# Windowed attention and two feed-forward blocks on one core: the first tile's tap sums and all weight-part sums move to TensorE

## Chip, cores and metric

The kernel runs on one core of a Trainium2 chip. The metric is the device time of one execution in microseconds (us); lower is better. Engines are named as in the profile: PE (TensorE matmul), PEld (its weight loads), DVE (VectorE), ACT (ScalarE), POOL (GpSimd), SP (SyncE, which issues all the DMAs here).

## What is computed

Three stages follow each other for 2 batches of 4160 tokens of width 192:

```python
# 1: every token is a weighted sum of itself and the 6 tokens before it
w = softmax(weight_gen, over its 7 taps)           # per token, head (8) and tap (7)
out[b, s, h, g] = sum_k w[b, s, h, k] * x_pad[b, s + k, h, g]
# 2: mix with the token before, then a gated feed-forward block, d_ff = 1024
xk = mu_k * x + (1 - mu_k) * x_prev ; xr = mu_r * x + (1 - mu_r) * x_prev
y  = sigmoid(xr @ w_r) * (relu(xk @ w_k) ** 2 @ w_v)
# 3: a second feed-forward block with a 3-tap convolution along the tokens
h  = relu(y @ w_in) ; c = conv3(h, conv_w) ; result = (h * sigmoid(c)) @ w_out
```

The mixing rates, the projections and the convolution weights of stages 2 and 3 arrive as 64-bit or 32-bit floats. A 64-bit matrix is read as pairs of 32-bit words.

## The kernel before

**Tiles.** The 4160 tokens of a batch are cut into 10 tiles (`SIZES`: 256, 220, seven of 476, 352). A tile is done for both batches. The loop at the end of `conv_moe_kernel` gives tile i the plan time T = 16 i; within it `moe1` and `moe2` run over 8 slices of the 1024 hidden units for each batch, and `moe2` lags `moe1` by 10 plan units, so that stage 3 works on the tile before while stage 2 works on this one.

**Order of the work.** No engine order is written by hand. Each step puts closures with a plan time into `plan` (`at`, line 292); they run in order of that time and append instructions to `prog.ops`. `Program.schedule` (line 106) then plays all instructions through a table of costs (`cost`, line 77), takes on each engine the ready instruction with the smallest plan time, and emits each engine's instructions in the order that this play gives. Each engine executes its list strictly in that order, so a changed cost or a moved instruction can change the order anywhere behind it. SP's list holds all the DMA issues.

**Stage 1** (`attention`, line 452). A tile's tokens lie on 128 partitions, in 2 to 4 slots each; one slot of one batch is a "token" below. For a token POOL multiplies the seven rows `rows` by the softmax weights `sw` into `prod` (128x1344, seven taps of 192) and adds the taps in three steps, the last of which writes `tok` (lines 466 to 470). There is one `prod` buffer. Tile 0 has four tokens, tile 1 has four, tile 2 and the later ones eight. The softmax weights are made ahead by `softmax` (line 421): DVE folds, ACT takes the exponential, and POOL subtracts and multiplies, these being the POOL instructions that write `sw`.

**Mixing** (`mixing`, line 481). PE transposes `tok` into a `pa` bank ("flip", the rows `pa<-ident,tok`); ACT copies the shifted tokens into `att`, DVE forms the mixture into `ar` or `mk`, ACT rounds its high part into `xA` or `rm`, and the low part is the rest (DVE for tile 0, POOL for later tiles). For a tile's unit u = 2, which needs the tokens of both batches, SP moves the parts into `xB` by DMA. Stage 2 of a batch starts with the matmuls `pa<-xA,wkA` and `pa<-xB,wkB`.

**Weights.** Each large matrix product is done in three passes of reduced-precision float32 parts ("high" and "low"). `prepare` (line 400) brings the weights in as 16 chunks; `fetch` loads one into `stage` by DMA (three buffers), `narrow` (line 321) makes a float32 value of the 64-bit words in a PSUM bank `px` (`bm` and `br` in turn), and `split` (line 345) rounds it to a high part and keeps the rest as the low part. For the first three chunks (`on_pe`, line 409) the sum of the two parts inside `narrow` is two matmuls with an identity matrix, `ident` (float32) and `signs` (rounded), and the subtraction inside `split` is a matmul with the negative identity followed by an ACT copy. For the other 13 chunks both are DVE instructions (lines 342 and 351). The `chunk_*` functions that say where a chunk goes all end in `split`, but for the convolution weights (`chunk_conv`).

**Store** (`store`, line 733). The result of the 64 last channels of a tile is put together in its own buffer `ob` and stored by DMA.

Of the kernel before, what the change touches and what calls it, by code (L numbers as in the profile page):

```python
# [1 line left out]

# [12 lines left out]
NB, SEQ, DM, NH, KS, DFF = 2, 4160, 192, 8, 7, 1024  # L15
# [12 lines left out]
WIN = KS * DM  # L28
# [6 lines left out]
def f(ap):  # L35
    return ap.bitcast(F32)


class Program:
# [37 lines left out]
    def cost(self, eng, method, out, ins, pointer):  # L77

        n = self.count(out)
        src = [self.space(x) for x in ins]  # L80
        if method == "dma_start":
            return 0.6, 0.0
        if eng == "PE":
            if method == "matmul" and ins[0].dtype == F32:
                n *= 4
            busy = max(n * 0.00045 + 0.002, 0.109)
            return busy, busy + 0.24
        if eng == "ACT":
            near = bool(src) and src[0] == "PSUM"
            p = 0.1 if pointer else 0.0  # L90
            return (0.06 if near else 0.09) + p + n / 1200, (0.2 if near else 0.24) + p + n / 1200
        if eng == "DVE":
            if method == "tensor_reduce":
                return 0.05 + self.count(ins[0]) / 515, 0.15 + self.count(ins[0]) / 515
            if method == "reciprocal":
                return 0.07 + n / 160, 0.2 + n / 160
            if method in ("tensor_scalar", "tensor_copy", "memset") and "PSUM" not in src:
                return 0.07 + n / 1920, 0.2 + n / 1920
            stt = method == "scalar_tensor_tensor"
            return (0.13 if stt else 0.07) + n / 960, (0.26 if stt else 0.2) + n / 960  # L100
        if eng == "POOL":
            busy = 0.15 + (n / 455 if method == "tensor_tensor" else n / 270)
            return busy, busy + 0.1
        return 0.6, 0.6
# [85 lines left out]
def conv_moe_kernel(ctx: ExitStack, tc: tile.TileContext, xp, wg_first, wg_rest, mus, w_k, w_v, w_r, w_in, conv_w, w_out, out):  # L190
    nc = tc.nc
    prog = Program(nc)
    PE, ACT, DVE, POOL, SP = (prog.engine(e) for e in ("PE", "ACT", "DVE", "POOL", "SP"))
# [3 lines left out]
    def new(name, shape, dtype=F32):  # L197
        t = sb.tile(shape, dtype, name=name)
        prog.spaces[t.tensor.name] = "SBUF"
        return t  # L200

    def ring(name, n, shape, dtype=F32):
        return Ring([new(f"{name}{j}", shape, dtype) for j in range(n)])

    def bank(name):
        t = ps.tile([128, 512], F32, name=name)
        prog.spaces[t.tensor.name] = "PSUM"
        return t

    W = NMAX + 4  # L210
# [22 lines left out]
    ident = new("ident", [128, 128])  # L233
# [12 lines left out]
    stage = new("stage", [128, 4096], U32)  # L246
# [5 lines left out]
    g_r = ring("g", 2, [128, 2, W], F32R)  # L252
    wz_r = Ring([t.rearrange("p a b -> p (a b)") for t in g_r.tiles])
    rows_r = ring("rows", 2, [128, max(SLOTS) + PAD, DM])
    prod = new("prod", [128, WIN])
    tok_r = ring("tok", 2, [128, max(SLOTS), NB * DM])
    att_r = ring("att", 2, [128, NMAX])
    mk_r = ring("mk", 2, [128, NMAX])
# [4 lines left out]
    s_r = ring("s", 2, [128, 2, NMAX], F32R)  # L263
    h_r = ring("h", 2, [128, W])
    om_r = ring("om", 1, [128, W])
    ob_r = ring("ob", 1, [64, W])


    slots = [NB * l for l in SLOTS]
    soft_at = [sum(slots[:j]) for j in (0, 1, 2, 3, NTILE)]  # L270
# [2 lines left out]
    sm = []  # L273
    for j in range(4):
        n = soft_at[j + 1] - soft_at[j]
        flat = new(f"smz{j}", [128, 2 * n * NH]) if j < 3 else f(stage)[:, :2 * n * NH]
        sm.append((sw[:, soft_at[j]:soft_at[j + 1]],
                   *(flat[:, c * n * NH:(c + 1) * n * NH].rearrange("p (s h) -> p s h", s=n) for c in (0, 1))))
    pa_r = Ring([bank(f"pa{j}") for j in range(2)])
# [10 lines left out]
    plan = []  # L290

    def at(t, fn, hold=0.0):
        plan.append((t, len(plan), fn, hold))

    def mm(dst, passes):
        n = len(passes)
        for i, (w, r) in enumerate(passes):
            PE.matmul(dst, lhsT=w, rhs=r, start=(i == 0), stop=(i == n - 1))
# [20 lines left out]
    on_pe = [False]  # L319

    def narrow(st, n):
        if not st["wide"]:
            return st["x"][:, :n]
        hi, lo = st["raw"][:, :n, 1], st["raw"][:, :n, 0]
        px, py = px_r()[:, :n], py_r()[:, :n]
        x, y, z = px.bitcast(U32), py.bitcast(U32), wy_r()[:, :n]
        ACT.activation(px, f(hi), ACTF.Copy, scale=2.0 ** -112)
        if on_pe[0]:

            zr = wz_r()[:, :n]  # L330
            DVE.tensor_scalar(x, x, 3, None, op0=ALU.logical_shift_left)
            DVE.scalar_tensor_tensor(out=z, in0=hi, scalar=0x80000000, in1=x, op0=ALU.bitwise_and, op1=ALU.bitwise_or)
            DVE.tensor_scalar(y, z, 0xFF800000, None, op0=ALU.bitwise_and)
            DVE.scalar_tensor_tensor(out=zr, in0=lo, scalar=2.0 ** -52, in1=py, op0=ALU.mult, op1=ALU.mult)
            PE.matmul(px, lhsT=ident, rhs=f(z), start=True, stop=False, skip_group_check=True)
            PE.matmul(px, lhsT=signs[:, 0:128], rhs=zr, start=False, stop=True, skip_group_check=True)
            return px
        DVE.tensor_scalar(x, x, 3, None, op0=ALU.logical_shift_left)
        DVE.scalar_tensor_tensor(out=x, in0=hi, scalar=0x80000000, in1=x, op0=ALU.bitwise_and, op1=ALU.bitwise_or)
        DVE.tensor_scalar(y, x, 0xFF800000, None, op0=ALU.bitwise_and)  # L340
        DVE.scalar_tensor_tensor(out=f(z), in0=lo, scalar=2.0 ** -52, in1=py, op0=ALU.mult, op1=ALU.mult)
        DVE.tensor_tensor(px, px, f(z), op=ALU.add)
        return px
# [56 lines left out]
    def prepare(first, seq):  # L400

        for j, (t, (load, n, go)) in enumerate(seq):
            st = {}

            def ld(st=st, load=load):
                st[0] = load()

            def use(st=st, n=n, go=go, j=j):
                on_pe[0] = j < 3
                go(narrow(st[0], n))  # L410

            at(first[j] if j < 3 else seq[j - 3][0] + 0.001, ld)
            at(t, use)
# [36 lines left out]
    rows_t, tok_t = {}, {}  # L450

    def attention(i, b, t_load, t, dt_, eng, hold=(0.0, 0.0)):
        L = SLOTS[i]

        def load():
            rows_t[i, b] = rows_r()[:, :L + PAD]
            row = b * (SEQ + PAD) + STARTS[i] - EXTRA[i]
            SP.dma_start(out=rows_t[i, b], in_=bass.AP(tensor=xp.tensor, offset=xp.offset + row * DM, ap=[[L * DM, PART[i]], [1, (L + PAD) * DM]]))

        def token(l):  # L460
            if i not in tok_t:
                tok_t[i] = tok_r()
            p = prod
            y = p.rearrange("p (k d) -> p k d", k=KS)
            w = sw[:, sum(slots[:i]) + b * L + l].unsqueeze(2).to_broadcast([128, KS, DM // NH, NH])
            eng.tensor_tensor(p.rearrange("p (k g h) -> p k g h", k=KS, h=NH),
                              rows_t[i, b][:, l:l + KS].rearrange("p k (g h) -> p k g h", h=NH), w, op=ALU.mult)
            eng.tensor_tensor(y[:, 0:3], y[:, 0:3], y[:, 3:6], op=ALU.add)
            eng.tensor_tensor(y[:, 0:2], y[:, 0:2], y[:, 2:7:4], op=ALU.add)
            eng.tensor_tensor(tok_t[i][:, l, b * DM:b * DM + DM], y[:, 0], y[:, 1], op=ALU.add)  # L470

        at(t_load, load, hold[0])
        for l in range(L):
            at(t + l * dt_, lambda l=l: token(l), hold[1])
# [258 lines left out]
    def store(i, b, t):  # L733
        N = UNIT[i]
        last = i == NTILE - 1
        a = 1 if i == 1 else 0
        n = N + (1 if last else 0)
        t0 = STARTS[i] - OFFSET[i] - 1
        st = {}

        def e0():
            st["b"] = ob_r()
            ACT.copy(st["b"][:, :n], acc2["r"][64:128, :n])

        def e1():
            st["m"] = om_r()
            ACT.copy(st["m"][:, :n], acc2["m"][:, :n])
            SP.dma_start(out=out[b, 0:128, t0 + a:t0 + n], in_=st["m"][:, a:n])

        def e2():  # L750
            DVE.tensor_tensor(st["b"][:, :n], acc2["r"][0:64, :n], st["b"][:, :n], op=ALU.add)
            SP.dma_start(out=out[b, 128:192, t0 + a:t0 + n], in_=st["b"][:, a:n])

        at(t, e0)
        at(t + 0.1, e1)
        at(t + 0.2, e2)
# [36 lines left out]
    for j in range(NTILE - 3):  # L793
        a, b = (sum(slots[3:3 + k]) for k in (j, j + 1))
# [10 lines left out]
    for i in range(NTILE):  # L805
# [6 lines left out]
        for b in range(NB):  # L812
            t = T + 8 * b
# [8 lines left out]
            if i:  # L822
                store(i, b, t + LAG + 10.02)

    for t, _, fn, hold in sorted(plan, key=lambda e: e[:2]):
        prog.now, prog.hold = t, hold
        fn()
    with tc.manual_schedule():
# [64 lines left out]
```

## Time and profile before

| | |
|---|---|
| median of 3 runs | 766.72 us (765.65 to 767.09) |
| the profiled execution, own time | 766.81 us |
| its span in the profile | 765.0 us |
| PE busy | 697.2 us (91%) |
| ACT busy | 650.8 us (85%) |
| DVE busy | 621.6 us (81%) |
| POOL busy | 506.6 us (66%) |

The profiled execution's own time is 1.8 us longer than its span. Busy times are shares of the whole span; the program is a start-up of some 45 us, then ten tiles in a pipeline, then an end. "Idle before <- X" in a row means that the engine stood still ahead of that instruction, and that X ended last among what it needed. A row of several instructions (x2, x3) gives the time from the first's start to the last's end. A float32 matmul with `ident` shows as two matmul records.

### The profile page before, as it was taken

To read this page: it belongs to the slowest core of one execution; us is meant where nothing else is said; L and a number is where in the kernel's file an instruction comes from. 1 tells how busy PE (TensorE), PEld (TensorE's weight loads), DVE (VectorE), ACT (ScalarE), POOL (GpSimd) and SP (SyncE) were. 2 spreads that over 40 slices of the span, in tenths; PEclk is the share of its full clock that TensorE was granted. 3 is DMA by queue.
4 is the path that set the end of the run, shared out by engine and by line. 5 is a ranking of instruction groups with operands and counts; after the bars stand their busy time and mean duration, and the time that the engine had idled before them with its cause. 6 is when DMAs were issued, how large, how long until landed. Compare 5 with 4: busy or idle time off the path is not lost.

```text
span 765.0 us, 10294 instructions
## 1 busy us (share of the span) xinstructions
PE 697.2 (91%) x3358; PEld 590.4 (77%) x3358; DVE 621.6 (81%) x1066; ACT 650.8 (85%) x1364; POOL 506.6 (66%) x362
## 2 busy tenths in 40 slices
PE   4177888998899999999999899999999999999996
PEld 1066676887677888887888688888888888888984
DVE  5897868877997979796979587888787878787887
ACT  3477779988888999898989798999899989898886
POOL 4999999999899999999999999585602010110000
PEclk9999999999999999999999999999999999999999
DMA  7768103012210140112120310120002000200000
GB/s 239 224 174 250 53 1 103 20 53 71 51 53 20 51 122 4 69 52 71 51 72 9 110 53 20 47 71 1 20 0 71 1 19 2 58 0 20 20 1 28
DMA packets 18788, 45.05 MB, mean 59 GB/s; under 512 B 2992, under 2 KB 14256, under 8 KB 18608
## 3 DMA queue, kind: packets, MB, share of 16 engines
q1 hardware_dynamic: 18736, 44.41, 19.4%
q8 instruction: 26, 0.43, 0.2%
q14 instruction: 26, 0.21, 0.1%
HBM read 27.40 MB, written 6.39 MB: 44 GB/s over the span
## 4 chain that ended last, share of the span: by engine, by line
POOL 43%; PE 40%; ACT 7%; issue 5%; DVE 2%; DMA 2%; SPq 0%; ACTq 0%; POOLq 0%
POOL prod L175 34%; PE pa L175 13%; PE pc L175 9%; PE bm L175 6%; PE am L175 6%; POOL tok L175 4%; PE br L175 4%; PE ar L175 3%; POOL xA L175 2%; POOL sw L175 1%; ACT pa L175 1%; POOL mk L175 1%; ACT pc L175 1%; ACT s L175 1%; DMA stage<-in_moe_w_k_dram 1%
## 5 line engine op out<-in xcount | busy, mean ns | idle before, releaser
L175 POOL TENSOR_TENSOR prod<-rows,sw 128x1344 f32<-128x1344 f32 x70 | 216.3, 3090 | 14.6 <-DVE sw L175 9.6
L175 DVE SCALAR_TENSOR_TENSOR pc<-h,cw,pc 128x476 f32<-128x476 f32 (+1 forms) x280 | 196.7, 703 | 30.2 <-ACT pc L175 27.5
L175 ACT ACTIVATE pa<-pa 128x476 f32<-128x476 f32 (+3 forms) x324 | 162.6, 504 | 40.9 <-PE pa L175 37.0
L175 POOL TENSOR_TENSOR prod<-prod 128x576 f32<-128x576 f32 (+1 forms) x140 | 171.0, 1221 | 9.5
L175 PE MATMUL am<-s,wv 128*128 128x476 f32 (+3 forms) x480 | 148.0, 366 | 9.3 <-ACT s L175 8.5
L175 PE MATMUL bm<-g,wo 128*128 128x476 f32 (+1 forms) x417 | 138.3, 379 | 6.4 <-ACT g L175 6.0
L175 PE MATMUL pa<-xA,wkA 128*128 128x476 f32 (+3 forms) x480 | 121.8, 361 | 8.3 <-DVE s L175 4.2
L175 DVE TENSOR_TENSOR pc<-h,pc 128x476 f32<-128x476 f32 (+1 forms) x140 | 90.0, 643 | 45.3 <-ACT pc L175 45.1
L175 PE MATMUL pc<-x,wiA 128*128 128x478 f32 (+1 forms) x420 | 116.1, 377 | 1.4 <-DVE g L175 1.2
L175 POOL TENSOR_TENSOR xA<-mk,xA 128x476 fp32r<-128x476 f32 (+2 forms) x36 | 40.1, 1122 | 109.4 <-ACT xA L175 81.6
L175 PE MATMUL ar<-s,wv 128*128 128x476 f32 (+3 forms) x320 | 110.8, 356 | 0.1
L175 DVE TENSOR_TENSOR s<-pa,s 128x476 fp32r<-128x476 f32 (+3 forms) x162 | 94.7, 586 | 19.6 <-ACT s L175 17.5
L175 PEld LDWEIGHTS am<-s,wv 128*128 128x128 f32 x480 | 87.7, 192 | 26.7 <-ACT s L175 15.8
L175 PE MATMUL br<-g,wo 128*128 128x476 f32 (+1 forms) x278 | 104.5, 376 | 0.0
L175 PEld LDWEIGHTS pa<-xA,wkA 128*128 128x128 f32 x480 | 85.2, 193 | 22.3 <-DVE s L175 6.5
L175 DVE TENSOR_TENSOR g<-pc,g 128x476 fp32r<-128x476 f32 (+1 forms) x137 | 87.9, 641 | 16.9 <-ACT g L175 16.6
L175 PEld LDWEIGHTS bm<-g,wo 128*128 128x128 f32 x417 | 76.9, 188 | 22.0 <-ACT g L175 10.3
L175 ACT ACTIVATE pc<-h,cw 128x476 f32<-128x476 f32 (+1 forms) x140 | 92.4, 660 | 1.5
L175 ACT ACTIVATE h<-pc 128x478 f32<-128x478 f32 (+1 forms) x140 | 79.8, 570 | 14.8 <-PE pc L175 11.8
L175 PE MATMUL pa<-xB,wkB 128*128 128x476 f32 (+3 forms) x320 | 88.8, 357 | 0.0
L175 PEld LDWEIGHTS pc<-x,wiA 128*128 128x128 f32 x420 | 76.0, 188 | 14.5 <-DVE g L175 3.8
L175 ACT CAST s<-pa 128x476 fp32r<-128x476 f32 (+3 forms) x162 | 83.4, 516 | 2.8 <-PE ar L175 0.8
(132 smaller groups left out, 1069.8 us busy)
## 6 DMA issues: line engine op xcount, KB each, us to landing
rows<-in_x_dram SPq DMA_DIRECT2D x14, 960.0 KB, 4.7
xB<-rm SPq DMA_DIRECT2D x28, 119.0 KB, 2.3
xB<-mk SPq DMA_DIRECT2D x28, 119.0 KB, 2.3
out_dram<-om SPq DMA_DIRECT2D x14, 238.0 KB, 2.0
rows<-in_x_dram SPq DMA_DIRECT2D x4, 768.0 KB, 6.2
rows<-in_x_dram SPq DMA_DIRECT2D x2, 864.0 KB, 4.3
out_dram<-ob SPq DMA_DIRECT2D x14, 119.0 KB, 2.2
stage<-in_moe_w_v_dram SPq DMA_DIRECT2D x4, 384.0 KB, 5.5
```

The costliest lines, as they stand in the source:

```text
L175: getattr(self.real[eng], method)(*a, **k)
```

## The change

What it does, part by part:

1. **Tile 0's tap sums on PE.** For the four tokens of tile 0 POOL does the multiplication alone. The seven taps are summed by seven float32 matmuls of 192 columns with `ident` into a `pa` bank, and ACT copies the bank into `tok`. `prod` becomes a ring of two buffers for all tiles.
2. **All chunks' sums on PE.** `on_pe` is true for all 16 chunks, so `narrow` and `split` use matmuls and ACT copies instead of DVE for the 13 others.
3. **Buffers.** The space for the second `prod` comes from three small softmax buffers, which now lie in the first `h` buffer, and from `ob`, whose place is now taken from the ring `att`.
4. **The planner.** A float32 matmul is costed at 4.6 instead of 4 columns' time, and a closure may put further closures into the plan while it runs (`later`; a heap in place of the sorted list). The cost only sets the order.

```diff
             if method == "matmul" and ins[0].dtype == F32:
-                n *= 4
+                n *= 4.6
...
-    prod = new("prod", [128, WIN])
+    prod_r = ring("prod", 2, [128, WIN])
...
-    ob_r = ring("ob", 1, [64, W])
...
-        flat = new(f"smz{j}", [128, 2 * n * NH]) if j < 3 else f(stage)[:, :2 * n * NH]
+
+        o = 2 * soft_at[j] * NH
+        flat = h_r.tiles[0][:, o:o + 2 * n * NH] if j < 3 else f(stage)[:, :2 * n * NH]
...
+    serial = [1 << 20]
+
+    def later(t, fn):
+        serial[0] += 1
+        heapq.heappush(plan, (t, serial[0], fn, 0.0))
...
             def use(st=st, n=n, go=go, j=j):
-                on_pe[0] = j < 3
+                on_pe[0] = j < 16
                 go(narrow(st[0], n))
...
-            p = prod
+            p = prod_r()
             y = p.rearrange("p (k d) -> p k d", k=KS)
...
+            if i < 1:
+
+                def total():
+                    z = pa_r()[:, :DM]
+                    for k in range(KS):
+                        PE.matmul(z, lhsT=ident, rhs=y[:, k], start=(k == 0), stop=(k == KS - 1))
+                    ACT.copy(tok_t[i][:, l, b * DM:b * DM + DM], z)
+
+
+                now = t + l * dt_
+                later((now + 0.2) // 1 + 0.8 if i else now, total)
+                return
             eng.tensor_tensor(y[:, 0:3], y[:, 0:3], y[:, 3:6], op=ALU.add)
...
         def e0():
-            st["b"] = ob_r()
+            st["b"] = att_r()[0:64]
...
-    for t, _, fn, hold in sorted(plan, key=lambda e: e[:2]):
+    heapq.heapify(plan)
+    while plan:
+        t, _, fn, hold = heapq.heappop(plan)
         prog.now, prog.hold = t, hold
```

**What it moves.** POOL's list at the start, from its first multiplication on (`rows_79` holds batch 0, `rows_80` batch 1; `smz_110` and `h_105` are softmax buffers). Before, the first token and the next one's multiplication:

```order
L175 TENSOR_TENSOR prod<-rows_79,sw 128x1344
L175 TENSOR_TENSOR prod<-prod 128x576
L175 TENSOR_TENSOR prod<-prod 128x384
L175 TENSOR_TENSOR tok_82<-prod 128x192
L175 TENSOR_TENSOR prod<-rows_79,sw 128x1344
```

Now, from the first token to the first multiplication of tile 1:

```order
L176 TENSOR_TENSOR prod_81<-rows_79,sw 128x1344
L176 TENSOR_TENSOR prod_82<-rows_79,sw 128x1344
L176 TENSOR_TENSOR sw<-sw,h_105 128x224
L176 TENSOR_TENSOR prod_81<-rows_80,sw 128x1344
L176 TENSOR_TENSOR prod_82<-rows_80,sw 128x1344
L176 TENSOR_TENSOR sw<-sw,h_105 128x224
L176 TENSOR_TENSOR sw<-sw,h_105 128x448 x2
L176 TENSOR_TENSOR prod_81<-rows_79,sw 128x1344
```

The three additions of each token are gone, and the four softmax instructions for tiles 1 and 2 now all stand ahead of tile 1's first token; before, the last of them stood behind it.

PE's list at the start, from the second chunk on (`br` and `bm` hold chunks, `pa_109` and `pa_110` are the two `pa` banks). Before:

```order
L175 MATMUL br<-stage,ident 128x512
L175 MATMUL br<-g_78,signs 128x512
L175 MATMUL br<-wkA,signs 128x512
L175 MATMUL bm<-stage,ident 128x384
L175 MATMUL bm<-g_77,signs 128x384
L175 MATMUL bm<-wv,signs 128x2x128
L175 MATMUL bm<-wv,signs 128x2x64
L175 MATMUL pa_112<-ident,tok_82 128x128 x2
```

Now:

```order
L176 MATMUL br<-stage,ident 128x512
L176 MATMUL pa_109<-prod_81,ident 128x192 x7
L176 MATMUL br<-g_78,signs 128x512
L176 MATMUL pa_110<-prod_82,ident 128x192 x7
L176 MATMUL br<-wkA,signs 128x512
L176 MATMUL bm<-stage,ident 128x384
L176 MATMUL pa_109<-ident,tok_83 128x128 x2
L176 MATMUL pa_110<-prod_81,ident 128x192 x7
L176 MATMUL bm<-g_77,signs 128x384
L176 MATMUL pa_109<-prod_82,ident 128x192 x7
L176 MATMUL bm<-wv,signs 128x2x128
```

The four groups of seven matmuls stand between the steps of the second and third chunk, and the flip of batch 0 stands ahead of the third group.

POOL's list between tile 2's last token and tile 3's first one. Before:

```order
L175 TENSOR_TENSOR tok_82<-prod 128x192
L175 TENSOR_TENSOR xA_90<-mk_86,xA_90 128x476
L175 TENSOR_TENSOR xA_92<-mk_87,xA_92 128x476
L175 TENSOR_TENSOR sw<-sw,stage 128x448 x2
L175 TENSOR_TENSOR mk_86<-mk_86,rm_88 128x476
L175 TENSOR_TENSOR sw<-sw,stage 128x448 x2
L175 TENSOR_TENSOR mk_87<-mk_87,rm_89 128x476
L175 TENSOR_TENSOR sw<-sw,stage 128x448
L175 TENSOR_TENSOR prod<-rows_79,sw 128x1344
```

Now:

```order
L176 TENSOR_TENSOR tok_83<-prod_82 128x192
L176 TENSOR_TENSOR xA_91<-mk_87,xA_91 128x476
L176 TENSOR_TENSOR xA_93<-mk_88,xA_93 128x476
L176 TENSOR_TENSOR sw<-sw,stage 128x448 x2
L176 TENSOR_TENSOR mk_87<-mk_87,rm_89 128x476
L176 TENSOR_TENSOR mk_88<-mk_88,rm_90 128x476
L176 TENSOR_TENSOR sw<-sw,stage 128x448 x5
L176 TENSOR_TENSOR prod_81<-rows_79,sw 128x1344
```

Seven softmax instructions stand here where five stood. The two came from places further on, one from ahead of tile 3's last token and one from behind it.

## Rows read from the trace of the kernel before

**Rows 1.** Busy time by stretch of the span, all engines.
```profile
core 0: us, PE busy (x) PEld busy (x) DVE busy (x) ACT busy (x) POOL busy (x), PEclk, DMA share, GB/s
...
10.00:46.00 36.00, 13.48 (x29) 6.86 (x29) 32.69 (x70) 17.56 (x47) 33.69 (x25) 1.00 0.71 203
46.00:83.00 37.00, 29.35 (x177) 25.98 (x178) 29.91 (x70) 27.19 (x80) 35.63 (x27) 0.95 0.62 185
83.00:130.00 47.00, 40.53 (x258) 34.31 (x257) 37.64 (x71) 37.82 (x96) 44.23 (x35) 1.00 0.17 55
...
435.00:735.00 300.00, 298.79 (x1445) 259.35 (x1443) 243.34 (x400) 272.68 (x557) 102.77 (x77) 1.00 0.10 27
```

**Rows 2.** Waits of PE over the whole span: total us, times, longest.
```profile
PE pa L175 <- POOL tok L175: 16.9, 3, 12.5
...
PE am L175 <- ACT s L175: 8.5, 14, 1.7
...
PE pa L175 <- DVE s L175: 4.2, 5, 1.7
```

**Rows 3.** POOL in order of time, start to tile 1: start, us, what.
```profile
10.98 3.04 POOL L175 TENSOR_TENSOR prod<-rows,sw 128x1344 f32<-128x1344 f32 x1 [9.63 <-DVE sw L175]
14.09 2.49 POOL L175 TENSOR_TENSOR prod<-prod 128x576 f32<-128x576 f32 x2
16.66 0.59 POOL L175 TENSOR_TENSOR tok<-prod 128x192 f32<-128x192 f32 x1
...
29.87 0.66 POOL L175 TENSOR_TENSOR sw<-sw,smz 128x224 f32<-128x224 f32 x1
...
38.39 3.04 POOL L175 TENSOR_TENSOR prod<-rows,sw 128x1344 f32<-128x1344 f32 x1
...
42.87 1.15 POOL L175 TENSOR_TENSOR sw<-sw,smz 128x448 f32<-128x448 f32 x1
```

**Rows 4.** PE in order of time, the start.
```profile
13.67 1.91 PE L175 MATMUL br<-stage,ident 128*128 128x512 f32 x2
...
36.79 1.11 PE L175 MATMUL pa<-ident,tok 128*128 128x128 f32 x4 [12.45 <-POOL tok L175]
...
43.66 1.15 PE L175 MATMUL pa<-xB,wkB 128*128 128x256 f32 x4
```

**Rows 5.** PE in order of time around 51.6 us.
```profile
51.40 0.41 PE L175 MATMUL ar<-s,wv 128*128 128x256 f32 x1
51.61 0.66 PE L175 MATMUL pa<-xA,wkA 128*128 128x256 f32 x3
```

**Rows 6.** ACT in order of time: a chunk's rounding and a softmax exponential.
```profile
28.83 0.58 ACT L175 CAST wkA<-bm 128x512 fp32r<-128x512 f32 x1 [1.43 <-DVE bm L175]
...
38.85 0.57 ACT L175 ACTIVATE sw<-sw 128x448 f32<-128x448 f32 x1
```

**Rows 7.** DVE in order of time: the two replaced steps of a chunk, a fold.
```profile
28.11 0.69 DVE L175 TENSOR_TENSOR bm<-bm,stage 128x512 f32<-128x512 f32 x1
...
29.77 0.68 DVE L175 TENSOR_TENSOR wkA<-bm,wkA 128x512 fp32r<-128x512 f32 x1
...
39.70 0.98 DVE L175 TENSOR_REDUCE smz<-sw 128x64 f32<-128x448 f32 x1
```

**Rows 8.** PE with long matmuls of stage 3, after 100 us.
```profile
112.68 0.81 PE L175 MATMUL pc<-x,wiA 128*128 128x478 f32 x3
```

**Rows 9.** POOL between tile 2 and tile 3.
```profile
121.78 2.25 POOL L175 TENSOR_TENSOR sw<-sw,stage 128x448 f32<-128x448 f32 x2
...
130.89 3.08 POOL L175 TENSOR_TENSOR prod<-rows,sw 128x1344 f32<-128x1344 f32 x1
```

**Rows 10.** PE, two of the waits after 130 us.
```profile
185.77 0.66 PE L175 MATMUL pa<-ident,tok 128*128 128x128 f32 x4 [1.97 <-POOL tok L175]
...
429.99 0.92 PE L175 MATMUL pa<-xA,wrA 128*128 128x476 f32 x3 [2.62 <-DVE mk L175]
```

**Rows 11.** The page's DMA issues: count, size, us to landing.
```profile
out_dram<-ob SPq DMA_DIRECT2D x14, 119.0 KB, 2.2
```

More of the change, by code (lines that the diff above doesn't have):

```diff
@@ L1 @@
+import heapq
 from contextlib import ExitStack
```

## The prediction

> **What bounds the kernel now.** I read the busy times by stretch first, then the waits of PE, then the two engines' lists at the start. The stretches [rows 1] show four regimes. From 10 to 46 us PE is busy 13.5 of 36 us, while DVE (32.7) and POOL (33.7) have hardly a gap: the start is paced by POOL's four tokens and by DVE's chunk preparation. From 46 to 130 us, where tiles 0 and 1 run, PE works 69.9 of 84 us and leaves 14.1 idle, with DVE at 67.5, ACT at 65.0 and POOL at 79.9 of 84. From 435 to 735 us PE is busy 298.8 of 300 us: there it is the bound, and POOL (102.8) is far ahead. In between PE has a few waits of 2 to 3 us [rows 10]. PE's largest sum of waits is on POOL's `tok`, 16.9 us, of which 12.5 us are one wait in the start; the next, on ACT's and DVE's `s`, are many small ones [rows 2]. So time can be gained in one piece at the start, when tile 0's tokens come earlier, and it is kept only if the pipeline behind it, POOL's list included, moves along by as much.
>
> **Part 1, the tokens.** A token costs POOL 3.04 for the multiplication, 2.49 for two additions and 0.59 for the third [rows 3], together 6.1 us. Without the additions a multiplication can follow each 3.1 us, but there are two buffers: the third multiplication waits until PE has read the first product.
>
> Seven matmuls of 192 columns are 1344 columns. A float32 `ident` matmul of 512 columns took 1.91 us [rows 4], so a sum takes at most 1344/512 x 1.91 = 5.0 us at that rate. That row lies at TensorE's lower clock level (1.2 GHz): matmuls still follow each other by 0.21 us for 256 columns up to 51.40 us, and get faster from 51.61 on [rows 5], after PE had run without gaps; later 478 columns take 0.27 each [rows 8], the upper level (2.4 GHz). The granted clock column reads 1.00 there [rows 1], so I go by the spacing. At the upper level a sum takes about half, 2.5 us. The trace has no such sum; these are the two ends. By the new list PE has no gap from the second chunk on, so I take the first sum at 5.0 and the others at 2.5.
>
> Step by step: the second chunk's `ident` matmul ends at 13.67 + 1.91 = 15.6. Sum 1 runs to 20.6, the chunk's next matmul (0.4) to 21.0, sum 2 to 23.5, the third chunk's two matmuls (0.9) and the flip (0.2) to 24.6. POOL's third multiplication starts when the first buffer is read, 20.6, and ends at 23.6, the fourth ends at 26.7. Sum 3 runs 24.6 to 27.1, sum 4 27.3 to 29.8. The ACT copy of 192 columns takes no more than the 0.58 of 512 [rows 6], so the last flip comes at about 30.4 instead of 36.79 [rows 4]: **6.4 us earlier**. From that flip to the first `xB` matmul were 6.9 us (43.66) of ACT, DVE and DMA steps that stay, so stage 2 starts 6.4 us earlier too. Batch 0's flip gains little, since sum 2 is late; but stage 2 waits for both batches.
>
> On POOL's list the fourth multiplication ends at 26.7. Then come the softmax pieces, 0.66 and 1.15 to 28.5, and the multiplication of tile 2's weights, which now stands ahead of tile 1's tokens and waits for an exponential and a fold: at least 0.57 + 0.98 us [rows 6, 7], at most 4.0, which is what lay between the exponential's start (38.85) and the multiplication (42.87 [rows 3]). I take the middle, 2.8, since DVE has less to do: it ends at 32.5, and tile 1's first token starts there instead of at 38.39, **5.9 us earlier** (4.7 to 7.1). POOL has hardly a gap from there to tile 3 [rows 1], so this travels with it. Between tiles 2 and 3 POOL now does seven softmax pieces where it did five, 1.12 us each (2.25 for two [rows 9]). One of the two comes from behind tile 3's last token, so at that token POOL's lead is 5.9 - 1.1 = **4.8 us** (3.6 to 6.0). There PE waited for POOL already, 1.97 us at 185.77 [rows 10]. A PE that comes there more than 4.8 us earlier waits longer, so POOL sets the gain.
>
> **Part 2, the chunks.** Of the 13 chunks four have 512 columns, eight 384 and one 24. One of 512 columns takes from DVE 0.69 + 0.68 us [rows 7]. It gives PE an `ident` matmul and two with `signs`: at the upper level 0.96 (half of 1.91) and 2 x 0.27 [rows 8], so 1.5, and 1.1 for 384 columns. ACT gets a second rounding of 0.58 [rows 6]. Two chunks come ahead of stage 2, where PE has room. The others, three of 512 and seven of 384, add 3 x 1.5 + 7 x 1.1 = **12.2 us to PE** between 46 and 130 us, where 14.1 are idle [rows 1]. With three quarters for a chunk of 384 columns they take about 11 from DVE's 67.5 (3 x 1.37 + 7 x 1.03) and add about 5 to ACT's 65.0. PE's waits there are on `s`, which ACT rounds and DVE subtracts [rows 2], and DVE's queue holds the chunk steps between these subtractions. I expect the shorter queue to bring `s` earlier, and PE to keep most of the 6.4 us: 4.8 or more at tile 3. If instead no idle time can be used, the stage grows by 12.2.
>
> The same edit makes PE wait, in its list, for a chunk's DVE and ACT steps, and what is queued behind is stage 2's matmuls; that is part of the rival below. On SP's list the loads of the gate weights now stand behind tile 0's `xB` copies and a load of tile 1's rows; I price this at nothing, since the gates come at the end of a batch.
>
> **Parts 3 and 4.** Taking the store's buffer from `att` costs nothing if the next use of that buffer comes after the DMA, 2.2 us [rows 11]. Uses by mixing and store alternate in the plan such that a store's buffer is wanted again seven plan units later, tens of microseconds. If that fails, ACT stands for up to 2.2 us per store. The softmax buffers lie in an `h` buffer that stage 3 uses only from 100 us on. The changed cost only orders.
>
> **The sum**, against the profiled execution's 766.81 us (0.1 above the median): -4.8, so **762.0 us** (760.8 to 763.2 from POOL's bounds).
>
> **The rivals.**
> - *The waits after 130 us shrink too.* POOL's and ACT's order is new everywhere, and the two waits shown make 1.97 + 2.62 = 4.6 us [rows 10]. If they go, and PE's lead of 6.4 us is not stopped at tile 3, the time is 766.8 - 4.8 - 4.6 = 757.4. Against it: new orders make new waits as easily.
> - *The sums stay at the lower clock* (slower). At 5.0 each, sum 2 ends at 26.0, sum 3 at 33.1, sum 4 at 38.5, and the last flip comes at 39.1, 2.3 us later than before: 769.1. It decides from the point where sums 2 to 4 take 4.6 instead of 2.5 us each. For it: PE works from 10 us on in the kernel before too, and with its gaps the matmuls are still at the lower level at 51.40 [rows 5]. Against it: the new list has no gaps. The Trainium skill, "TensorE: Matmul & The Clock Gate", section "HAM oscillation", adds that idle gaps bring the clock back down. By that rule sums would be slow wherever PE stands between them, as in this rival; the trace agrees so far that 46 to 83 us, where PE has gaps, has a mean granted clock of 0.95 [rows 1].
> - *PE is filled up* (slower). If the 12.2 us of chunk matmuls, with their waits for DVE and ACT in PE's list, do not fit between tile 0's and 1's matmuls, the start's 6.4 us are paid back and 5.8 more: 772.6. It decides where more than half of the 12.2 lengthens the stage. For it: ACT would be at 70 of 84 us, and PE at 82. Against it: DVE, fuller than ACT in the first of these two tiles' stages (29.9 of 37 [rows 1]), loses 11.
> - *Nothing much changes.* Half of the 12.2 us lengthens the stage: about 766.5.
>
> **The numbers.** What a measurement can tell from no change is 0.2%, 1.5 us. The forecast has 0.52, the smaller waits 0.17, no change 0.12, the lower clock 0.08, the filled PE 0.11. Faster is 0.69, same 0.12, slower 0.19. The range from 755.5 to 770.5 leaves out most of the filled PE and a gain beyond the second case.
>
> **What would show it.** Right: POOL's tile 0 shows multiplications alone, the fourth ending near 27; the last flip near 30; stage 2's first `xB` matmul near 37; tile 1's first multiplication near 32.5; DVE's busy time down by about 14 us, PE's idle time between stage 2's start and tile 2 well under 14. Wrong: four sums of 5 us each, or long waits `PE bm <- DVE` or `PE br <- ACT` in tile 0, or a wait of PE for `tok` near 181 that is much longer than 2 us.

## The result and the profile after

The changed kernel takes **759.99 us** (median of 4 runs, 759.34 to 760.33), the kernel before 766.71 beside it: a ratio of 0.991, 95% interval 0.9894 to 0.9926, 6.7 us. The forecast was 762.0 with a range of 755.5 to 770.5. The profiled execution has a span of 757.9 us against 765.0, so 7.1 us are to be found in the traces. The busy times, from the page of the changed kernel:

```profile
PE 715.6 (94%) x3473; PEld 607.1 (80%) x3473; DVE 606.8 (80%) x1033; ACT 656.6 (87%) x1388; POOL 492.4 (65%) x350
```

DVE lost 14.8 us, POOL 14.2; PE gained 18.4. By stretch (columns as in [rows 1]):

```profile
10.00:46.00 36.00, 32.15 (x143) 24.83 (x144) 25.72 (x53) 20.73 (x60) 30.13 (x17) 0.91 0.71 197
46.00:83.00 37.00, 30.77 (x182) 23.59 (x180) 24.09 (x54) 29.55 (x88) 34.57 (x29) 1.00 0.69 197
83.00:130.00 47.00, 41.12 (x258) 34.99 (x256) 38.28 (x71) 39.28 (x101) 45.03 (x33) 1.00 0.20 61
435.00:735.00 300.00, 297.39 (x1442) 257.97 (x1440) 245.65 (x407) 272.26 (x560) 95.39 (x71) 1.00 0.09 25
```

The start is what the forecast said it would be: PE busy 32 of 36 us, where it was busy 13.5. From 46 to 130 us PE works 71.9 us instead of 69.9 and is still idle for 12.1. PE in order of time in the start, and POOL:

```profile
15.44 3.83 PE L176 MATMUL pa<-prod,ident 128*128 128x192 f32 x14
19.34 2.44 PE L176 MATMUL pa<-prod,ident 128*128 128x192 f32 x14
...
22.70 2.44 PE L176 MATMUL pa<-prod,ident 128*128 128x192 f32 x14
25.49 2.54 PE L176 MATMUL pa<-prod,ident 128*128 128x192 f32 x14 [0.18 <-POOL prod L176]
...
28.64 0.60 PE L176 MATMUL pa<-ident,tok 128*128 128x128 f32 x4
...
36.05 0.63 PE L176 MATMUL pa<-xB,wkB 128*128 128x256 f32 x2
```

```profile
11.05 6.03 POOL L176 TENSOR_TENSOR prod<-rows,sw 128x1344 f32<-128x1344 f32 x2 [9.70 <-DVE sw L176]
...
19.40 6.04 POOL L176 TENSOR_TENSOR prod<-rows,sw 128x1344 f32<-128x1344 f32 x2 [1.71 <-issue]
25.40 1.76 POOL L176 TENSOR_TENSOR sw<-sw,h 128x224 f32<-128x224 f32 x2
29.79 1.14 POOL L176 TENSOR_TENSOR sw<-sw,h 128x448 f32<-128x448 f32 x1 [2.64 <-DVE h L176]
30.88 3.04 POOL L176 TENSOR_TENSOR prod<-rows,sw 128x1344 f32<-128x1344 f32 x1
```

The last flip comes 8.2 us earlier than in [rows 4], stage 2's first `xB` matmul 7.6 us, tile 1's first multiplication 7.5 us earlier than in [rows 3].

**The lead along the program.** How much of that is kept is read by taking the same instruction in both traces. DVE writes the low part of `s` 162 times and ACT makes `h` from `pc` 140 times; the start of the n-th one before, less its start after, is the lead there. For the 19th `s`, from DVE's list in order of time of the kernel before and of the changed one:

```profile
87.86 0.37 DVE L175 TENSOR_TENSOR s<-pa,s 128x220 fp32r<-128x220 f32 x1
```

```profile
87.73 0.38 DVE L176 TENSOR_TENSOR s<-pa,s 128x220 fp32r<-128x220 f32 x1
```

0.13 us: of the 7.6 us, nothing is left 88 us into the program. Read the same way for every kernel of this study (lead over the kernel before in us, one profiled execution of each; the columns are named in the next section):

| place (time before) | changed | e1 | e5 | e6 | e2 | e3 | e4 | e7 | e8 | e9 | e10 | e11 | e12 |
|---|---|---|---|---|---|---|---|---|---|---|---|---|---|
| first `s`, 46.2 | 7.6 | -0.2 | -0.5 | 8.7 | 8.6 | -1.7 | 8.4 | 8.6 | 8.8 | 6.9 | 8.3 | 4.4 | 7.0 |
| 13th `s`, 74.6 | 5.1 | -0.8 | -1.1 | 5.4 | 4.0 | -2.5 | -0.7 | 5.1 | 6.7 | 3.6 | 4.8 | 2.2 | 4.5 |
| 19th `s`, 87.9 | 0.1 | -0.7 | -1.1 | 0.4 | -0.4 | -3.2 | -5.7 | -1.5 | 1.2 | -3.2 | -0.2 | -2.2 | 3.3 |
| first `h`, 102.7 | 0.2 | -0.8 | -1.2 | 0.4 | -1.6 | -2.9 | -5.6 | -2.0 | 0.8 | -3.1 | -11.3 | -3.0 | 3.5 |
| `h`, 253.0 | 2.3 | -0.1 | -1.2 | 1.6 | 0.6 | -2.5 | -3.3 | 1.3 | 3.7 | -1.2 | -13.4 | 0.3 | 1.1 |
| `h`, 371 | 4.0 | 1.6 | -1.1 | 1.7 | 0.3 | -0.8 | -1.7 | 2.9 | 3.5 | 0.4 | -11.8 | 2.0 | 2.7 |
| `h`, 448 | 7.1 | 4.5 | 0.4 | 1.7 | 0.7 | 1.9 | 1.2 | 6.0 | 4.0 | 3.3 | -8.8 | 4.8 | 5.8 |

From 448 us on nothing changes in any column by more than 0.2 us. So the 7.1 us come in three late steps: about 2.2 between 103 and 253 us, 1.7 near 350 and 3.1 near 425. For the most part they are waits of PE that became shorter; near 425 us some 1.5 us are TensorE's clock (last section). From 175 to 260 us PE waits, before and after:

```profile
PE bm L175 <- ACT g L175: 2.1, 3, 1.4
PE pa L175 <- POOL tok L175: 2.0, 1, 2.0
PE pa L175 <- ACT r L175: 1.8, 1, 1.8
PE pc L175 <- DVE g L175: 1.0, 2, 0.7
```

```profile
PE am L176 <- ACT s L176: 4.4, 2, 4.0
PE bm L176 <- ACT g L176: 0.2, 1, 0.2
```

6.9 us became 4.6. The wait for `tok` of [rows 10] is gone. The new order has a wait of 4.0 us for ACT at 185 us in its place, while POOL itself stands. Near 350 us the kernel before has a wait of 1.4 us, and the changed kernel has none there. PE of the kernel before:

```profile
351.53 0.92 PE L175 MATMUL pa<-xA,wrA 128*128 128x476 f32 x3 [1.39 <-DVE mk L175]
```

The wait at 430 us of [rows 10] is 1.0 us instead of 2.6. The changed kernel's PE, then POOL, in order of time:

```profile
185.31 1.01 PE L176 MATMUL am<-s,wv 128*128 128x476 f32 x2 [4.03 <-ACT s L176]
...
424.40 0.91 PE L176 MATMUL pa<-xA,wrA 128*128 128x476 f32 x3 [1.01 <-DVE mk L176]
```

```profile
186.85 1.19 POOL L176 TENSOR_TENSOR xA<-mk,xA 128x476 fp32r<-128x476 f32 x1 [8.55 <-ACT xA L176]
```

Two questions follow. What removed the late waits, if the start's lead was gone by then? And what spent that lead?

### The profile page after: what moved, and what is told of

It is laid out like the page before. It is cut to its first block, busy times and chain, and to the rows that moved or that the text cites. A ratio compares the mean times of both kernels' runs of the same rounds, so it can differ in the third digit from the quotient of the medians.

```text
span 757.9 us, 10505 instructions
## 1 busy us (share of the span) xinstructions
PE 715.6 (94%) x3473; PEld 607.1 (80%) x3473; DVE 606.8 (80%) x1033; ACT 656.6 (87%) x1388; POOL 492.4 (65%) x350
## 4 chain that ended last, share of the span: by engine, by line
PE 59%; POOL 20%; ACT 11%; DVE 6%; issue 3%; DMA 1%; SPq 0%; ACTq 0%; POOLq 0%; DVEq 0%
PE pa L176 18%; POOL prod L176 16%; PE pc L176 13%; PE bm L176 9%; PE am L176 8%; PE br L176 5%; PE ar L176 5%; ACT pa L176 2%; POOL tok L176 2%; ACT pc L176 2%; DVE pc L176 1%; POOL xA L176 1%; DVE stage L176 1%; ACT h L176 1%; ACT att L176 1%
## 5 line engine op out<-in xcount | busy, mean ns | idle before, releaser
L176 POOL TENSOR_TENSOR prod<-prod 128x576 f32<-128x576 f32 (+1 forms) x132 | 161.6, 1224 | 8.8
L176 PE MATMUL am<-s,wv 128*128 128x476 f32 (+3 forms) x480 | 145.4, 362 | 8.3 <-ACT s L176 8.2
L176 PEld LDWEIGHTS am<-s,wv 128*128 128x128 f32 x480 | 86.3, 188 | 24.8 <-ACT s L176 14.1
L176 PEld LDWEIGHTS pc<-x,wiA 128*128 128x128 f32 x420 | 76.2, 188 | 13.5 <-DVE g L176 2.5
```

The source lines that it names most:

```text
L176: getattr(self.real[eng], method)(*a, **k)
```

## The experiments

Each kernel was timed in three rounds against the kernel before on the same chip. Beside them the median of before was 767.2 to 767.8 us, so the ratios say more than the differences.

### e1 to e4: which part of the change

The first expectations speak of **Lead** (what the start wins is carried along POOL's list and removes the later waits), **Order** (the engines' new lists remove them) and **Front** (what counts happens in tiles 0 and 1).

**e1_neutral**: the buffers and the planner's cost alone. Tap sums stay on POOL, and three chunks stay on PE:

```diff
-                on_pe[0] = j < 16
+                on_pe[0] = j < 3
...
-            if i < 1:
+            if i < 0:
```

> The changed kernel with both edits of work taken back (the taps of tile 0 on POOL, three chunks on PE), so that only the buffers and the planner's cost are left. Three theories. 'Lead': the gain of 6.7 us comes from POOL's lead of 7.5 us at the start, which the pipeline uses up later, between 180 and 435 us. 'Order': the waits after 180 us went because the planner dealt another order. 'Front': the gain is PE's earlier start of stage 2, carried to the end. Lead and Front expect the time of before, 766.7 plus or minus 1; Order expects it too if the order stays the same, and any gain here would be the buffers'.

762.0 us, ratio 0.9924 (0.9899 to 0.9949). PE's, DVE's and ACT's lists have the order of the kernel before, POOL's too up to about 460 us. Lead and Front, which expected 766.7, fail: a kernel with no edit of the work has most of the gain. It has no lead at 46 us, and the steps near 350 and 425 us.

**e2_tokens**: `j < 3` alone, so the tap sums are on PE and the chunks as before.

> The changed kernel with three chunks on PE as before: tile 0's taps on PE alone. Lead: POOL's lead of about 7.5 us at tile 1 is there, and PE is not filled with 11 us of chunk matmuls, so at stage 3's start (101 us before) PE leads by 4 us or more, where the changed kernel leads by 0.2; the end is at 758 to 761, as the changed kernel. Front: the whole lead is carried and the end is at 759 or lower only if PE leads there. Order: anything from 757 to 768, with waits in new places. If the chunks' move matters for the gain, this ends above 763.

766.19 us, ratio 0.998 (0.9965 to 0.9995), not the 758 to 761 of Lead. The lead of 8.6 us at 46 us is gone at 88 us without any added chunk matmul.

**e3_chunks**: `if i < 0` alone, so all chunks are on PE and the tap sums on POOL.

> The changed kernel with tile 0's taps on POOL: all chunks on PE alone. Lead: POOL has no lead (tile 1's first multiplication at 38 plus or minus 1), PE gets about 12 us more work between 46 and 100 us, and stage 3 starts 0 to 6 us later than before; the time is 766 to 772. Front: no earlier flip, so 766.7 or later. Order: 760 to 772. A time under 764 would say that DVE's relief pays by itself.

765.07 us, ratio 0.9968 (0.9956 to 0.9981), earlier than Lead and Front allow. The chunks by themselves cost 3 us up to 103 us; the late steps bring more than that.

**e4_poollate**: the changed kernel's lists, with a memset and six additions put ahead of tile 1's first multiplication on POOL, so that POOL gives back its lead:

```diff
+        nc.gpsimd.memset(spare, 0.0)
+        for _ in range(6):
+            nc.gpsimd.tensor_tensor(spare, spare, spare, op=ALU.add)
```

> The changed kernel, every engine's order unchanged, with one memset and six additions of 480 columns on POOL in a buffer that is not in use yet, right ahead of tile 1's first multiplication: about 7.3 us of delay, which takes POOL's lead away and nothing else. Lead: the waits between 180 and 435 us come back and the time is 764 to 768. Order and Front: the order and the flip at 29 us are as in the changed kernel, so it stays at 760 plus or minus 1.5.

766.27 us, ratio 0.999 (0.9978 to 1.0003). POOL in order of time, then PE:

```profile
30.42 0.50 POOL L858 MEMSET om<- 128x480 f32 x1
31.00 6.31 POOL L860 TENSOR_TENSOR om<-om 128x480 f32<-128x480 f32 x6
37.27 3.06 POOL L181 TENSOR_TENSOR prod<-rows,sw 128x1344 f32<-128x1344 f32 x1
```

```profile
62.47 0.44 PE L181 MATMUL pa<-ident,tok 128*128 128x128 f32 x2 [3.13 <-POOL tok L181]
```

POOL, some 6.4 us later than in the changed kernel, makes PE wait 3.1 us for tile 1's tokens, and at 88 us its lead is 5.8 us below the changed kernel's. Yet the steps at 350 and 425 us are there (from -3.3 to 1.2 us). They depend neither on the start's lead nor on the new lists, since e1 has the old ones. Lead and Order both fall for these steps. What e1 and e4 share is the buffers and the planner's cost, which only orders.

### e5 and e6: the second `prod` buffer

From here on **Ring** is the theory that the second `prod` buffer does it.

**e5_oneprod**: e1 with `ring("prod", 1, ...)`. On every engine its order is that of the kernel before.

> The buffers' kernel (no edit of the work: tap sums on POOL, three chunks on PE, the new homes of the softmax and store buffers, the new cost), but with one prod buffer again; the order on every engine is that of the kernel before. Ring (the second prod buffer lets POOL begin each multiplication 0.1 us sooner, and by 350 and 425 us that puts POOL ahead of two waits of PE): the time goes back to 766.7 (766 to 767.5), and PE's wait of 2.6 us at 430 is there again. Buffers (another of the moved buffers brings it): stays at 762.0.

766.46 us, ratio 0.9988 (0.9974 to 1.0002): the gain is gone. So the other moved buffers and the cost bring and cost nothing that can be told from zero. POOL's list in order of time, in e5 and in e1:

```profile
17.14 0.59 POOL L176 TENSOR_TENSOR tok<-prod 128x192 f32<-128x192 f32 x1
17.81 3.03 POOL L176 TENSOR_TENSOR prod<-rows,sw 128x1344 f32<-128x1344 f32 x1
...
24.14 3.02 POOL L176 TENSOR_TENSOR prod<-rows,sw 128x1344 f32<-128x1344 f32 x1
```

```profile
17.00 0.60 POOL L176 TENSOR_TENSOR tok<-prod 128x192 f32<-128x192 f32 x1
17.56 3.03 POOL L176 TENSOR_TENSOR prod<-rows,sw 128x1344 f32<-128x1344 f32 x1
...
23.77 3.03 POOL L176 TENSOR_TENSOR prod<-rows,sw 128x1344 f32<-128x1344 f32 x1
```

With one buffer a multiplication begins 0.08 us after the end of the addition that reads the buffer, with two 0.04 us before that end. A token takes 6.33 instead of 6.21 us. That is only 0.12 us, but from 38 to 440 us POOL has few gaps (the longest, 3.6 us, at 194 us in both kernels) and works through 52 tokens before the wait at 430 us: at most some 6 us. There POOL's list has a multiplication of 3.1 us ahead of the `xA` for which DVE's `mk` waits, and behind `mk` the matmul of [rows 10]. In e5 that multiplication starts at 424.80, in e1 at 420.65, so 4.15 us are there. PE in e5 shows the old wait, in e1 less than half of it:

```profile
431.10 0.91 PE L176 MATMUL pa<-xA,wrA 128*128 128x476 f32 x3 [2.62 <-DVE mk L176]
```

```profile
426.97 0.91 PE L176 MATMUL pa<-xA,wrA 128*128 128x476 f32 x3 [1.18 <-DVE mk L176]
```

The sum closes: POOL is 4.15 us earlier in e1, PE 2.7 (1.6 and -1.1 at 371 us in the table), and the wait is shorter by the difference, 1.44.

**e6_prodfirst**: the changed kernel, the second buffer for tile 0 alone. On PE, DVE and ACT the order is the changed kernel's.

```diff
-            p = prod_r()
+            p = prod_r() if i == 0 else prod_r.tiles[0]
```

> The changed kernel with the same order on every engine; the second prod buffer serves tile 0 alone, later tokens use one buffer. Ring: the steps at 350 us (1.7) and 425 us (3.0) go, the rest of the gain stays: 764.7 (763.5 to 766). Lead (what is gained in the start is carried through and the second buffer matters only in tile 0): 760.0.

765.61 us, ratio 0.9976 (0.996 to 0.9992). The steps at 350 and 425 us are gone, a lead of 1.7 us is left in the trace. POOL's order differs from the changed kernel's only from 452 us on, behind both steps. **Ring holds** in both directions: the second buffer for the later tiles is worth 0.0064 in the old order (e1 against e5) and 0.0066 in the new one (the changed kernel against e6), some 5 us, and all the rest of the change 0.0024 (e6).

The buffer alone is not enough, though. e2 has it and lacks both steps, and PE waits 1.70 us at 351 and 2.19 at 429. Its POOL list, put in another order by the planner, has a multiplication between the two `xA`. POOL of e2 in order of time:

```profile
344.50 1.21 POOL L176 TENSOR_TENSOR xA<-mk,xA 128x476 fp32r<-128x476 f32 x1
345.67 0.59 POOL L176 TENSOR_TENSOR tok<-prod 128x192 f32<-128x192 f32 x1
346.23 3.10 POOL L176 TENSOR_TENSOR prod<-rows,sw 128x1344 f32<-128x1344 f32 x1
349.30 1.18 POOL L176 TENSOR_TENSOR xA<-mk,xA 128x476 fp32r<-128x476 f32 x1
```

In e1, with the old order, there is none between these two. This points to two conditions: where POOL's list puts its 3.1 us pieces, and how far ahead POOL is. The first was not tested by itself.

### e7 to e9: what spends the start's lead

In the changed kernel four chunks (12 to 15, one of `w_in` and three of `w_out`) are made between 72 and 90 us, where the lead falls from 5.1 to 0.1. **Filled** says that their matmuls on PE spend it, **Chain** that loads or the steps on ACT and DVE do.

**e7_chunk12** and **e8_chunk8**: the changed kernel with `j < 12` and `j < 8`, so the last four or eight chunks are back on DVE.

> The changed kernel with chunks 12 to 15 (the four of w_out, 384 columns each, done near 66 to 90 us) back on DVE. Filled (PE's added chunk matmuls between 75 and 88 us pay back the lead of 7.6 us): PE loses 4 x 1.1 us there, so some 4 us of the lead are left at 100 us, and up to that much at the end: 756 to 758. Chain (the lead ends against something that does not move, such as ACT's and DVE's steps for tile 1 or the chunks' loads): lead at 100 us still under 1 us, 759.5 to 761.5.

760.77 us, ratio 0.9918 (0.989 to 0.9946), which can't be told from the changed kernel's. (Chunk 12 is one of 512 columns of `w_in`; the expectation takes all four for `w_out`.)

> The changed kernel with chunks 8 to 15 back on DVE: PE loses some 9 us of chunk matmuls from 60 us on, DVE gets 8 us. Filled: the lead at 100 us is 4 to 7 us, time 755 to 758. Chain: under 1 us, as with four chunks, 759.5 to 762. Dve (DVE's chunk steps delay its subtractions, as in the tokens-alone kernel): lead at 100 us below zero, 761 to 766.

763.05 us, ratio 0.995 (0.9933 to 0.9967). Taking the matmuls off PE leaves no lead worth having: -1.5 and 1.2 us at 88 us. What Filled expected does not come, but both kernels also put DVE's steps back and have new orders, so they do not decide alone. e8's time lies in the range of Dve, its lead of 0.8 us at 103 us does not.

**e9_bare**: the changed kernel, order kept, some 10 us of PE's chunk matmuls (chunks 7 to 15, at the prediction's prices) left out:

```diff
+            if i in self.drop:
+                continue
...
+        if bare[0]:
+            prog.drop.add(len(prog.ops))
+        PE.matmul(*a, **k)
...
+                bare[0] = j >= 7
```

> The changed kernel, every engine's order kept, with PE's identity matmuls of chunks 7 to 15 left out (the weights of these chunks lack the sum of their two parts and their exact low part; DVE's and ACT's steps and the loads stay). PE loses some 10 us between 46 and 90 us. Filled (the matmuls on PE pay back the start's lead of 7.6 us): lead at 100 us 5 us or more, and since POOL waited 8.6 us for ACT at 187 us it follows: 755 to 757. Chain (loads, ACT's and DVE's chunk steps end the lead, PE's time for them fits into idle time): lead at 100 us under 2 us, 758.5 to 760.5.

764.35 us, ratio 0.9948 (0.9931 to 0.9966). With less work it is *slower* than the changed kernel, by 0.38% or some 3 us (3.8 between the traces), which neither theory had. PE's waits of e9 in order of time, then the first of these matmuls in the changed kernel:

```profile
79.28 1.01 PE L178 MATMUL pa<-xA,wkA 128*128 128x256 f32 x3 [2.85 <-DVE s L178]
...
87.36 0.98 PE L178 MATMUL pa<-xA,wkA 128*128 128x220 f32 x3 [2.07 <-DVE s L178]
```

```profile
77.77 0.62 PE L176 MATMUL pa<-xA,wkA 128*128 128x256 f32 x3 [0.24 <-DVE s L176]
```

And the stretch from 75 to 90 us, in the changed kernel, then in e9 (the granted clock stands behind POOL's column):

```profile
75.00:90.00 15.00, 12.54 (x73) 9.22 (x72) 12.78 (x28) 10.89 (x39) 14.57 (x13) 1.00 0.26 94
```

```profile
75.00:90.00 15.00, 9.10 (x39) 8.11 (x40) 11.45 (x25) 9.27 (x32) 13.41 (x12) 0.58 0.26 93
```

DVE's chunk steps hold up its subtractions, PE stands, and the granted clock falls to 0.58 of full speed, so for most of the stretch TensorE is at its lower level (1.2 GHz). Three matmuls of 256 columns take 1.01 us where they took 0.62 in the changed kernel. There the chunk matmuls stand in just these waits, and while PE works through them the clock stays at 1.00. In e7 it is 0.61 in this stretch, in e8 0.66, in e2 0.61. Not all of e9's loss falls here: by the table it is 0.7 us behind the changed kernel at 46 us, 1.5 at 75 us, 3.3 at 88 us and 3.8 at the end. The Trainium skill, "TensorE: Matmul & The Clock Gate", section "HAM oscillation", has TensorE throttled again where it stands between bursts of matmuls. The traces of e2, e7, e8 and e9 agree with that; e5 has a wait of 2.62 us at 430 us behind which the clock stays at 1.00 (last section).

### e10 and e11: a shorter list for POOL

**e10_soft4** and **e11_soft2**: the softmax subtractions and multiplications of tiles 3 to 6, or of tile 2, on DVE.

```diff
-        softmax(3, a, b, POOL, ...
+        softmax(3, a, b, DVE if j < 4 else POOL, ...
```

> The changed kernel with the softmax subtractions and multiplications of tiles 3 to 6 on DVE instead of POOL; POOL loses some 9 us in all between 110 and 420 us. Ring (what is won at 350 and 425 us is POOL being early enough, and 1.0 us of a wait is still there): at least that 1 us goes, 757.5 to 759.5. Full (POOL is early enough now and DVE's queue pays): 760 to 763.

773.93 us, ratio 1.0078 (1.0057 to 1.0099), far outside both expectations. The planner brought the moved pieces, and with them an exponential between two table loads of 1.28 us each on ACT, forward from 113 to 123 us to 90 to 96 us. ACT's gate sigmoid comes behind them, at 95.65 us, and PE waits for it:

```profile
96.06 0.98 PE L176 MATMUL pa<-xA,wrA 128*128 128x220 f32 x3 [3.23 <-ACT r L176]
```

The clock is 0.79 from 90 to 100 us and 0.73 from 100 to 130. The run says nothing about Ring or Full, since the order moved.

> The changed kernel with tile 2's softmax steps on DVE, so that POOL does not stand for 2.6 us ahead of tile 1's first multiplication and loses 2.3 us of work. Lead (POOL's list sets the time through tile 3): POOL 4 to 5 us earlier at tile 1, 756 to 757. Filled (PE and the chunks pay back what the start wins up to 88 us): lead at 100 us unchanged within 1 us, 759 to 761.

762.31 us, ratio 0.9922 (0.9897 to 0.9948). DVE's longer list delays the start: PE waits 1.74 us for DVE's `stage` ahead of the last tap sum, the lead at 46 us is 4.4 instead of 7.6 us, and -3.0 at 103 us. POOL begins tile 1 at 28.23 instead of 30.88 us, then stands 4.23 us at 45 us for `rows` by DMA. Neither theory had this; the move costs more at the start than POOL gains.

### e12: the chunk steps

**e12_nosteps**: as e9, but only for chunks 12 to 15 (`j >= 12`), and with DVE's four steps left out too.

> The changed kernel, every engine's order kept, with DVE's four steps and PE's three or more matmuls of chunks 12 to 15 left out (these four chunks hold only a rounded copy of the high words); their loads and ACT's copies stay. Steps (the lead of 5 us at 74.6 us is spent on these chunks' steps on DVE and PE): lead at 88 us 4 us or more, and at 100 us too, time 755 to 757.5. Clock (without the chunk matmuls PE's clock falls to its lower level between 75 and 90 us, as when only PE's share was left out): lead at 88 us 0 to -4, 760 to 765. Elsewhere (ACT's order or the loads end it): lead at 88 us 0 to 1 with the clock at 1.00, 759.5 to 761.

760.33 us, ratio 0.9899 (0.9877 to 0.992). The lead at 88 us is 3.3, and 3.5 at 103 us, where e9, in which only PE's share is left out, has -3.2 and -3.1. How DVE's steps spend it can be read at the 15th `s`, where the changed kernel's lead falls from 5.1 to 1.9. ACT's rounding of this `s` and DVE's subtraction, in the changed kernel, then in e12:

```profile
73.88 0.37 ACT L176 CAST s<-pa 128x256 fp32r<-128x256 f32 x1
77.30 0.41 DVE L176 TENSOR_TENSOR s<-pa,s 128x256 fp32r<-128x256 f32 x1
```

```profile
74.52 0.37 ACT L178 CAST s<-pa 128x256 fp32r<-128x256 f32 x1
74.93 0.42 DVE L178 TENSOR_TENSOR s<-pa,s 128x256 fp32r<-128x256 f32 x1 [3.04 <-ACT s L178]
```

In the changed kernel DVE comes to it 3.05 us after ACT's end, behind seven chunk steps in a row from 73.30 us on; in e12 0.04 us after. So **these chunks' steps on DVE spend most of the lead**. The 4 us expected are not reached, and the time expected for Steps is missed by 3 us: the lead that is kept does not get through. In e12's order of time PE meets this:

```profile
111.78 1.11 PE L178 MATMUL pa<-ident,tok 128*128 128x128 f32 x4 [3.09 <-POOL tok L178]
```

That is tile 2's last token. POOL's list has hardly a gap up to there, as in the changed kernel, where the same token ends at 111.18 us and the flip follows at 111.86 without a wait. So POOL is a second cap right behind the first. Between 103 and 253 us e12 loses 2.4 us of lead where the changed kernel gains 2.2. Of these 4.6 the wait is 3.1, and a granted clock of 0.94 from 100 to 130 us has a part in the rest, which was not followed further.

No version of this study beats the changed kernel; e12, at about its time, leaves work out.

## Why the prediction was right, and where not

The time is 2.0 us below the forecast and well inside the range. The way there was another one, and the hit is in good part luck: of the forecast's -4.8 us some 1.8 are left (e6), and some 5 us came from a buffer that was costed at nothing.

- **The tap sums on PE: right, a little better.** Sum 1 took 3.83 us instead of 5.0, since the clock rose within it, the others 2.44 to 2.54 instead of 2.5. The fourth multiplication ended at 25.4 (26.7 foretold), the last flip came at 28.64 (30.4), stage 2's first `xB` matmul at 36.05 (37). The rival of the lower clock is out for these sums.
- **Tile 1's first multiplication: right in kind.** 30.88 us against 32.5, a lead of 7.5 us, above the 4.7 to 7.1 given. POOL's wait of 2.64 us for the fold is the one foreseen.
- **"PE to keep most of the 6.4 us": wrong.** This is the step that failed in part 2. The lead was 7.6 us at 46 us and 0.1 at 88 us. The working compared sums over 84 us (12.2 us of matmuls against 14.1 us of idle time) and took from DVE what the edit takes from it, without asking what is left ahead of each `s`: at 73 us seven of the steps that stay on DVE stand ahead of one, and it comes 3.05 us late. From 75 to 90 us DVE is 12.8 of 15 us busy even with the edit. On the matmuls the step was right, they run while PE would wait; that the kernel is slower without them (e9) it did not have.
- **"Nothing much changes"** is what parts 1 and 2 come to: e6, the change without the second buffer for later tiles, gains 0.24%. The lead was paid back, as in the rival of the filled PE, but not the 5.8 us more, and to DVE's steps, not to PE's.
- **POOL's cap at tile 3: not what sets the time.** No wait for `tok` is left at 181 to 186 us, and POOL stands 8.55 us there. POOL does cap the lead at tile 2's last token (e12), and its lead is needed at tile 1 (e4), but neither bounds the changed kernel at tile 3.
- **Part 3 at nothing: wrong for one of its buffers.** The other buffers cost and bring nothing that can be told from zero (e5). The second `prod` buffer was looked at only where POOL waits for PE's sums. For the later tiles it shortens a token by 0.12 us, 52 times before 430 us, and that brings 0.64 to 0.66% (e1 against e5, the changed kernel against e6), more than the whole rest of the change. The rows for it were there: in [rows 3] each instruction that needs the one before it starts some 0.08 us after that one's end (14.09 + 2.49 = 16.58, next 16.66). I did not ask which of these dependences the ring removes.
- **The rival "the waits after 130 us shrink too" came true** in part: the wait for `tok` at 186 us went, and the one at 430 us fell from 2.62 to 1.01. It was given 0.17, and new orders as its cause. At 430 us the old order does as well, since the wait is 1.18 us in e1. The 4.0 us at 185 us are the new wait that spoke against it. It had also built on the lead of the start, which was spent.
- **The signs**: DVE's busy time fell by 14.8 us (about 14 foretold). PE's idle time between 46 and 130 us is 12.1, not well under 14; that was the sign that would have told of the lost lead.

## What to carry to other kernels

A lead won early is worth nothing until one has followed the same instruction in both traces to the place where it ends: here 7.6 us were gone 40 us later. On an engine that is full for hundreds of microseconds, ask of every second buffer which dependences between neighbours it removes, and multiply the tenth of a microsecond by the count up to the next wait that hangs on that engine. Work on PE that falls into PE's waits can be worth more than nothing, since taking it out can lower the clock of the work that stays.

## What the runs showed of the hardware

- On POOL a multiplication into a buffer that the addition before it reads starts 0.08 us after that addition's end, into another buffer 0.04 us before it (e5 and e1): 0.12 us for one such dependence.
- Leaving out some 10 us of matmuls made the kernel 0.38% slower (e9 against the changed kernel), with a granted clock of 0.58 instead of 1.00 from 75 to 90 us.
- The same wait of 2.62 us came with two prices. From 430 to 435 us, in the kernel before and in e5, with the same order:

```profile
430.00:435.00 5.00, 5.00 (x16) 4.26 (x17) 3.47 (x6) 3.87 (x8) 4.76 (x4) 0.66 0.43 99
```

```profile
430.00:435.00 5.00, 3.90 (x18) 3.31 (x19) 3.54 (x6) 4.91 (x10) 4.77 (x5) 1.00 0.43 99
```

  The clock is 0.66 in the one and 1.00 in the other, and e5 gains 1.5 us of lead there without any wait getting shorter (-1.1 to 0.4). So of the changed kernel's 3.1 us at this place 1.6 are the shorter wait and about 1.5 the clock. In the other traces, e10 and its late lists left out, PE waits for this `mk` between 423 and 431 us. Where it is 1.0 to 1.4 us long (the changed kernel, e1, e3, e4, e7, e9, e11, e12), the clock stays at 1.00 from 425 to 435 us. Where it is 2.2 to 2.6 us long, the clock falls in four of five: to 0.66 in the kernel before, 0.68 in e2 and 0.71 in e6 from 430 to 435 us, to 0.66 in e8 from 425 to 430 us. So here the shorter wait saves the clock's part as well. What spares e5 stays open.
